# Output-projection weights of a cached-attention decode block loaded in four sets of heads, with attention outputs dealt to the rows by identity products

## The chip, the cores and the metric

The kernel runs on one core of one Trainium2 chip. The metric is the time of one execution in microseconds (us) of device time. A core has a matrix engine (TensorE, "PE" in the profile, with its weight loads shown apart as "PEld"), a vector engine (VectorE, "DVE"), an activation engine (ScalarE, "ACT"), a general engine (GpSimd, "POOL") and a small engine that here only issues transfers (SyncE, "SP"). Sixteen DMA engines carry the transfers between the off-chip memory (HBM) and the on-chip memory: SBUF with 128 partitions, into which DMA can write, and PSUM, into which the matrix engine writes.

## The reference

A decode step of one token for four batch rows: an attention block over a cache, then a gated MLP, each with a normalised input that is scaled, shifted and gated by six vectors made from `c`. Cut to what matters:

```python
B, Sq, D = 4, 1, 512
H, Sk, Dh = 32, 4096, 128

def _A_ref(x, k_cache, v_cache, wq, wo):
    q = (x @ wq).reshape(B, Sq, H, Dh).transpose(0, 2, 1, 3)
    scores = einsum('bhqd,bhkd->bhqk', q, k_cache) * Dh ** (-0.5)
    p = softmax(scores)
    o = einsum('bhqk,bhkd->bhqd', p, v_cache)
    return o.transpose(0, 2, 1, 3).reshape(B, Sq, H * Dh) @ wo

mod = (silu(c) @ w_mod).reshape(4, 6, 1, -1)      # sa, ca, ga, sb, cb, gb
h = layernorm(x) * (1 + ca) + sa
x = x + ga * _A_ref(h, A_k_cache, A_v_cache, A_wq, A_wo)
h = layernorm(x) * (1 + cb) + sb
return x + gb * _B_ref(h, ...)                    # gelu, layernorm, gate, two matmuls
```

All arrays are bf16. The K cache and the V cache have 4 x 32 x 4096 x 128 elements each, 134 MB each. `A_wo` is 4096 x 512, 4.2 MB; the rows of one head are 128 neighbouring rows.

## The kernel before

**Tiling.** The work on the cache is cut into 32 tiles (`NT`). Tile `i` is one batch row `b = i % 4` and one group `g = i // 4` of four heads (`HQ = 4`), so that a K tile `kt` and a V tile `vt` are each 128 partitions x 32 KB, 4 MB. A quarter of the partitions (32) belongs to each of the four heads. Two buffers each of `kt` and `vt` exist; the last V tile takes a buffer of `kt`.

**Per tile.** VectorE multiplies a K tile in place by the query, in two halves (`mult`, line 279). TensorE sums the products over the head dimension by products with the identity into PSUM (`reduce_d`, line 285), VectorE adds the last eight (`sum8`), finds the maximum (`scores`), ScalarE takes the exponential into `pbd`, a block-diagonal arrangement of the probabilities. TensorE multiplies it with the V tile (`pv`, line 354); VectorE picks the wanted blocks (`o_pick`, lines 362 and 366), TensorE turns the result into columns (`o_cols`), and VectorE divides by the softmax sum (`o_scale`, into `oTs`). The softmax sum itself is made by `norm_r`, `norm_a` (TensorE) and `norm_b` (a reciprocal on VectorE).

**The order.** It is written out by hand: the loop at the end of the kernel body issues, for every `i`, the first half of tile `i`, `scores(i - 1)`, `norm_b(i - 2)`, the last steps of tile `i - 3`, the second half of tile `i`, and `pv(i - 2)`. Each engine runs its instructions in that order.

**Transfers.** All large loads are issued by SP, one after the other, on one queue, in this order: `w_mod`, `A_wq`, K 0, K 1, V 0; then in each turn `load_k(i + 2)` after the second `reduce_d` of tile `i` and `load_v(i)` after `pv(i - 2)`. A load waits in SP until its buffer is free. At `i == 2`, when `w_mod` and `A_wq` are used up, the pool that held them is closed and another is opened in the same place; the weights of the output projection go there (line 482 `wo_sb` for the first 28 heads, line 485 `wo_last` for the last four). At `i == 30` the last V tile is loaded in four pieces (`TAIL`), followed by the two MLP weights.

**The output projection before.** The 28 heads of `wo_sb` lie in pairs: two heads have 256 rows of `A_wo`, and partition `p` holds rows `2p` and `2p + 1` of the pair, a run of 2 KB in HBM:

```python
in_=A_wo[0:hl].rearrange("(t p r) n -> p t r n", p=P, r=2)
```

So partition `p` of a pair holds, for the first head, the dimensions `2p` and `2p + 1` if `p < 64`, and of the second head if `p >= 64`. The columns of the attention output have to stand the same way: for a tile of the first seven groups `o_cols` makes four products, each with every second column of `osb`, into 64 partitions, and `norm_b` makes two reciprocals, one per half of the partitions. `oTs` has room for `[2, 2]` values per tile and partition (row `r`, pair `t`). Once a group has its four batch rows, `project` runs `o_proj`: 16 products of 128 x 128 weights with four columns, summed over the four heads, and `add_up` adds the result to `acc` in the next turn. The last group and its weights `wo_last` stand head by head, without pairs.

**The end.** After the loop the last V tile is multiplied piece by piece (`o_last`, line 390) while the residual, the second layer norm and the MLP follow; `gate` (line 585) needs `win_sb`, and the last product needs `wout_sb`.

Of the kernel before, what the change touches and what calls it, by code (L numbers as in the profile page):

```python
# [8 lines left out]
BF16 = mybir.dt.bfloat16  # L9
F32 = mybir.dt.float32  # L10
AF = mybir.ActivationFunctionType
ALU = mybir.AluOpType
AX = mybir.AxisListType
PSUM = bass.MemoryType.PSUM

HQ = 4
KC = 64
RD = 8
TAIL = (64, 32, 16, 16)


@with_exitstack
def kernel(
# [16 lines left out]
    nc = tc.nc  # L40
    P = 128
    B, _, D = A_x.shape
    _, H, SK, DH = A_k_cache.shape
    F = B_w_in.shape[1]
    FH = F // 2
    DJ = D // P
# [3 lines left out]
    NQ = H // HQ  # L50
    NT = B * NQ
    R = P // HQ
# [5 lines left out]
    L = NT - 1  # L58
    BL = B - 1
# [3 lines left out]
    consts = ctx.enter_context(tc.tile_pool(name="consts", bufs=1))  # L63
    kvp = ctx.enter_context(tc.tile_pool(name="kv", bufs=2))
    wk = ctx.enter_context(tc.tile_pool(name="work", bufs=2))
    psum = ctx.enter_context(tc.tile_pool(name="psum", bufs=1, space=PSUM))
# [4 lines left out]
    def ps_sm(shape, dtype=F32):  # L71
        return psum.tile(shape, dtype, name="sm", bufs=3)
# [36 lines left out]
    def load_v(i):  # L109
# [8 lines left out]
    ident_bf = consts.tile([P, P], BF16, name="ident_bf")  # L118
    make_identity(nc, ident_bf)
    ident_f = consts.tile([P, P], F32, name="ident_f")  # L120
# [19 lines left out]
        out=sel32, in_=ident_f.rearrange("p (q r) -> p r q", r=R), axis=AX.X, op=ALU.add  # L140
# [8 lines left out]
    sel4 = consts.tile([P, HQ], F32, name="sel4")  # L149
    idr = ident_f.rearrange("p (c g q) -> p g c q", g=R // HQ, q=HQ)  # L150
    for g in range(G):
        nc.vector.tensor_reduce(out=selg[:, g:g + 1], in_=idr[:, g], axis=AX.XY, op=ALU.add)
    nc.vector.tensor_reduce(
        out=sel4, in_=ident_f.rearrange("p (c b) -> p b c", b=B), axis=AX.X, op=ALU.add
    )
    acc = consts.tile([P, DJ, B], F32, name="acc")
    nc.vector.memset(acc, 0.0)
    x1w = consts.tile([P, DJ, R], F32, name="x1w")
# [3 lines left out]
    for k in range(3):  # L162
        t = consts.tile([P, NJ, HQ], BF16, name=f"pbd{k}")
        nc.gpsimd.memset(t, 0.0)
        pbds.append(t)
    for k in range(2):
        t = psum.tile([P, G, DH], F32, name=f"ops{k}", bufs=1)
# [26 lines left out]
    def normed(pool, src, name, then=None, last=None):  # L194
# [24 lines left out]
        out=sg, in0=cx, scalar1=-60.0, scalar2=-1.0, op0=ALU.max, op1=ALU.mult  # L219
# [6 lines left out]
    def mod_cols(s0, n, dst, m0=0, blocks=False):  # L226
# [21 lines left out]
        out=hs, in0=modA[:, DJ:2 * DJ, :], scalar=1.0, in1=xn, op0=ALU.add, op1=ALU.mult  # L248
# [22 lines left out]
    queries(0)  # L271

    st = {}
    oTs = consts.tile([P, NT, 2, 2], BF16, name="oTs")

    def mult(i, kc):
        kt = kts[i][:, kc * KC:(kc + 1) * KC, :]
# [54 lines left out]
        nc.tensor.matmul(z, lhsT=ones_f, rhs=st.pop((i, "rsb")), start=True, stop=True)  # L332
        st[i, "z"] = z

    def norm_b(i):
        rz = wk.tile([P, 2, 2], F32, name="rz", bufs=3)
        z = st.pop((i, "z"))
        if i // B == NQ - 1:  # L340
            nc.vector.reciprocal(out=rz, in_=z.rearrange("p (r t) -> p r t", t=2))
        else:
            for a in range(2):
                h = slice(64 * a, 64 * (a + 1))
                nc.vector.reciprocal(out=rz[h, 0, :], in_=z[h, a:HQ:2])  # L345
            rz = rz[:, 0:1, :].to_broadcast([P, 2, 2])
        st[i, "rz"] = rz

    def pv(i):
# [20 lines left out]
        st[i, "osb"] = osb  # L370

    def o_cols(i):
        op = ps_sm([P, 2, 2])
        osb = st.pop((i, "osb"))
        if i // B == NQ - 1:
            nc.tensor.matmul(op, lhsT=osb, rhs=sel4, start=True, stop=True)
        else:
            for a in range(2):
                for r in range(2):
                    nc.tensor.matmul(  # L380
                        op[64 * a:64 * (a + 1), r, :], lhsT=osb[:, r:P:2],
                        rhs=sel4[:, a:HQ:2], start=True, stop=True, tile_position=(0, 64 * a),
                    )
        st[i, "op"] = op

    def o_last(i, part):
        if part == 0:
            st[i, "op"] = psum.tile([P, 2, 2], F32, name="qps", bufs=1)
        for k in range(sum(TAIL[:part]), sum(TAIL[:part + 1])):
            nc.tensor.matmul(  # L390
                st[i, "op"], lhsT=vts[i][:, k, :], rhs=pbds[i % 3][:, k, :],
                start=(k == 0), stop=(k == NJ - 1),
            )
# [3 lines left out]
            out=oTs[:, i], in0=st.pop((i, "op")), in1=st.pop((i, "rz")), op=ALU.mult  # L397
        )

    def o_proj(g, b0, b1):  # L400
        wp = ps_sm([P, DJ, b1 - b0])
        for j in range(DJ):
            for q in range(HQ):
                r, t = divmod(q, 2)
                w = wo_last[:, q, :] if g == NQ - 1 else wo_sb[:, g * 2 + t, r, :]
                nc.tensor.matmul(
                    wp[:, j, :], lhsT=w[:, j:D:DJ], rhs=oTs[:, g * B + b0:g * B + b1, r, t],
                    start=(q == 0), stop=(q == HQ - 1),
                )
        return wp  # L410

    def o_add(wp, b0, b1):
        a = acc[:, :, b0:b1]
# [8 lines left out]
    spf = consts.tile([P, 2], F32, name="spf")  # L422
    adds = []

    def project(i):

        if i >= 0 and i % B == BL and i < L:
            adds.append((o_proj(i // B, 0, B), 0, B))

    def add_up():  # L430
        while adds:
            o_add(*adds.pop(0))

    QPLAN = {0: (1, 2), 1: (3, 4, 5), 2: (6, 7)}
    for i in range(NT):
        more = list(QPLAN.get(i, ()))
        mult(i, 0)
        if i >= 1:
            scores(i - 1)
        if i >= 2:  # L440
            norm_b(i - 2)
        add_up()
        if i >= 3:
            o_pick(i - 3)
        reduce_d(i, 0)
        if i >= 3:
            o_cols(i - 3)
        if more:
            queries(more.pop(0))
        mult(i, 1)  # L450
        if i >= 1:
            norm_r(i - 1)
        if i >= 3:
            o_scale(i - 3)
        sum8(i, 0)
        reduce_d(i, 1)
        load_k(i + 2)
        if i >= 1:
            norm_a(i - 1)
        project(i - 3)  # L460
        while more:
            queries(more.pop(0))
        if i >= 2:
            pv(i - 2)
        if i == 0:
            load_v(1)
        elif 2 <= i < L:
            load_v(i)
        if i == 2:
            nc.scalar.dma_start(out=sp_t[:, 0:1], in_=B_w_sp[0:1, 0:1])  # L470
            nc.scalar.dma_start(out=sp_t[:, 1:2], in_=B_b_sp.rearrange("(a b) -> a b", b=1))
            mps = ps_sm([P, 4 * DJ, B])
            mod_cols(2, 3 * DJ, mps)
            mod_cols(5, DJ, mps, 3 * DJ, True)
            nc.vector.tensor_copy(out=modT, in_=mps[:, 0:3 * DJ, :])
            nc.vector.tensor_copy(out=gsT, in_=mps[:, 3 * DJ:, :])
            pre_cm.__exit__(None, None, None)
            wts = tl = ctx.enter_context(tc.tile_pool(name="wts", bufs=1))
            wo_sb = wts.tile([P, H // 2 - 2, 2, D], BF16, name="wo_sb")
            wo_last = wts.tile([P, HQ, D], BF16, name="wo_last")  # L480
            hl = (H - HQ) * DH
            nc.sync.dma_start(
                out=wo_sb, in_=A_wo[0:hl].rearrange("(t p r) n -> p t r n", p=P, r=2)
            )
            nc.sync.dma_start(out=wo_last, in_=A_wo[hl:H * DH].rearrange("(q p) n -> p q n", p=P))
        if i == 5:
            sps = ps_sm([P, 2])
            nc.tensor.matmul(sps, lhsT=ones_b, rhs=sp_t, start=True, stop=True)
            nc.vector.tensor_copy(out=spf, in_=sps)
            nc.vector.tensor_scalar(  # L490
                out=gwT, in0=gsT, scalar1=spf[:, 0:1], scalar2=None, op0=ALU.mult
            )
            nc.vector.tensor_scalar(
                out=gsT, in0=gsT, scalar1=spf[:, 1:2], scalar2=None, op0=ALU.mult
            )
            nc.vector.tensor_copy(out=g8[:, :, 1, :], in_=gwT.rearrange("p j b -> p b j"))
            cbT = modT[:, 2 * DJ:3 * DJ, :]
            nc.vector.tensor_scalar_add(out=cbT, in0=cbT, scalar1=1.0)
        if i == L - 1:
            load_v(L)  # L500
            win_sb = wts.tile([P, DJ, F], BF16, name="win_sb")
            nc.sync.dma_start(out=win_sb, in_=B_w_in.rearrange("(p j) n -> p j n", p=P))
            wout_sb = wts.tile([P, NH, D], BF16, name="wout_sb")
            nc.sync.dma_start(out=wout_sb, in_=B_w_out.rearrange("(j p) n -> p j n", p=P))
# [13 lines left out]
    o_pick(L - 1)  # L518
    o_cols(L - 1)
    o_scale(L - 1)  # L520
    adds.append((o_proj(NQ - 1, 0, BL), 0, BL))
    add_up()
    o_last(L, 0)


# [3 lines left out]
    def sums():  # L529
# [2 lines left out]
        o_scale(L)  # L532

    xc, rs2 = normed(tl, x1, "ln2", lambda: o_last(L, 1), sums)
    wp = o_proj(NQ - 1, BL, B)
    last = tl.tile([P, DJ], F32, name="last")
    nc.vector.tensor_tensor(out=last, in0=wp[:, :, 0], in1=gaT[:, :, BL], op=ALU.mult)
    xs = st2[:, 0, 0:DJ]
# [13 lines left out]
        out=nv2, in0=mq2[:, 0:1], scalar=mq2[:, 0:1], in1=mq2[:, 1:2],  # L552
        op0=ALU.mult, op1=ALU.subtract,
# [4 lines left out]
    hl = tl.tile([P, DJ], F32, name="hl")  # L558
    nc.vector.scalar_tensor_tensor(
        out=hl, in0=xs, scalar=mq2[:, 0:1], in1=cbT[:, :, BL], op0=ALU.subtract, op1=ALU.mult  # L560
    )
    nc.vector.scalar_tensor_tensor(
        out=hT2[:, :, BL], in0=hl, scalar=rsl, in1=sbT[:, :, BL], op0=ALU.mult, op1=ALU.add
# [4 lines left out]
        out=x1m, in0=x1[:, :, :, None].to_broadcast([P, DJ, B, HQ]),  # L568
        in1=mask4[:, None, None, :].to_broadcast([P, DJ, B, HQ]), op=ALU.mult,
    )  # L570
    x1r = ps_sm([B * DJ, P])
    for k in range(DJ):
        nc.tensor.matmul(
            x1r[:, k:P:DJ], lhsT=x1m[:, k].rearrange("p b j -> p (b j)"), rhs=sel32,
            start=True, stop=True,
# [4 lines left out]
    def gate(h):  # L580
# [22 lines left out]
        in1=st3[:, 0:2], op=ALU.mult,  # L603
# [72 lines left out]
```

## Time and profile before

| what | value |
|---|---|
| time, median of 3 runs | 670.07 us (669.81 to 670.64) |
| the profiled execution | 671.33 us |
| its span, first to last instruction | 669.5 us |
| busy: PE, PEld, DVE, ACT, POOL | 403.3, 181.8, 421.1, 85.0, 3.8 us |
| read from HBM | 282.73 MB, 422 GB/s over the span |
| granted TensorE clock, mean | 0.828 |

The profile is of one execution. It has a page and answers to further questions. On the page, part 2 cuts the span into 40 equal slices: a digit is the busy share of a slice in tenths, and under `DMA` it is the mean of the 16 DMA engines; `GB/s` is what they moved. Part 3 lists the DMA queues with packets, MB and the share of the sixteen engines' time. Part 4, the chain, follows the work that ended last backwards from step to step and gives the share of each engine and line. Part 5 has the groups of instructions: line, engine, operation, output and inputs, count, then busy time, mean ns of one, idle time before and its cause. A line `L285` is line 285 of the kernel. The table of stretches gives for each stretch its length, busy time (and instruction count) of PE, PEld, DVE, ACT and POOL, the granted clock, the DMA share and GB/s. The timeline gives start, duration, engine, line, operation and, in brackets, the idle time before it and what ended it. The trace also records every DMA packet with its size and how long it took.

### The profile page before, as it was taken

How to read it: one execution, taken by the hardware profiler on the slowest of the kernel's cores; microseconds unless marked ns; L12 is line 12 of the kernel's file. 1: busy time of each engine (PE TensorE's matmuls, PEld its weight loads, DVE VectorE, ACT ScalarE, POOL GpSimd, SP SyncE). 2: the span in 40 equal slices, each digit the busy share in tenths (PEclk: the TensorE clock that was granted, in tenths of full speed). 3: DMA queues.
4: the chain of work that ended last, by engine and by line, in shares of the span. 5: the costliest groups of instructions: out<-in, count | busy, mean ns of one | idle time of the engine just before them, and what ended most of it. 6: DMA issues, size and time to landing. Idle time of an engine off the chain costs nothing.

```text
span 669.5 us, 7043 instructions
## 1 busy us (share of the span) xinstructions
PE 403.3 (60%) x2920; PEld 181.8 (27%) x2920; DVE 421.1 (63%) x614; ACT 85.0 (13%) x278; POOL 3.8 (1%) x17
## 2 busy tenths in 40 slices
PE   1185886365676576557655664675565467555666
PEld 1032432122232232223222222232222233222325
DVE  3186494765666776666677665567766666776833
ACT  1011111110111111001111100111111011111112
POOL 1000000000000000000000000000000000000000
PEclk9999877678888777898877689878778897877975
DMA  9999999999999999999999999999999999999994
GB/s 376 437 426 435 400 404 418 433 439 428 430 433 434 435 432 431 432 435 434 430 433 431 434 434 433 430 431 432 437 432 435 426 436 433 435 434 422 435 422 198
DMA packets 13555, 283.18 MB, mean 423 GB/s; under 512 B 1228, under 2 KB 2644, under 8 KB 4692
## 3 DMA queue, kind: packets, MB, share of 16 engines
q1 hardware_dynamic: 13504, 282.73, 98.6%
q8 instruction: 23, 0.38, 0.2%
q14 instruction: 8, 0.07, 0.0%
q10 hardware_dynamic: 20, 0.01, 0.0%
HBM read 282.73 MB, written 0.00 MB: 422 GB/s over the span
## 4 chain that ended last, share of the span: by engine, by line
DMA 58%; DVE 28%; PE 13%; issue 1%; SPq 0%; ACT 0%; DVEq 0%
DMA kt<-in_A_k_cache_dram 52%; DVE kt L279 20%; PE red L285 11%; DMA win_sb<-in_B_w_in_dram 5%; DVE osb L366 2%; DVE S L294 1%; DVE osb L362 1%; DVE mrow L303 1%; PE ops L354 1%; DVE rz L345 1%; DVE mt L307 0%; PE qps L265 0%; DVE nM L309 0%; DVE mb L305 0%; DVE nM L310 0%
## 5 line engine op out<-in xcount | busy, mean ns | idle before, releaser
L285 PE MATMUL red<-kt,ident_bf 128*128 128x512 bf16 x1024 | 302.3, 461 | 234.7 <-DVE kt L279 234.7
L279 DVE TENSOR_TENSOR kt<-kt,qbc 128x8192 bf16<-128x8192 bf16 x64 | 282.8, 4420 | 191.7 <-DMA kt<-in_A_k_cache_dram 190.7
L285 PEld LDWEIGHTS <-ident_bf 128*128 128x128 bf16 x1024 | 116.3, 114 | 408.7 <-issue 284.9
L317 ACT ACTIVATE pbd<-S,nM 32x128 bf16<-32x128 f32 x128 | 73.8, 576 | 504.9 <-DVE nM L310 463.6
L354 PE MATMUL ops<-vt,pbd 128*16 128x512 bf16 x992 | 60.7, 387 | 0.2 <-DMA vt<-in_A_v_cache_dram 0.2
L294 DVE TENSOR_REDUCE S<-red 128x64 f32<-128x512 f32 x64 | 43.7, 682 | 6.3 <-PE red L285 6.3
L366 DVE SCALAR_TENSOR_TENSOR osb<-ops,selg,osb 128x128 f32<-128x128 f32 x93 | 32.6, 351 | 3.3
L317 ACT ACTIVATION_READ_ACCUMULATOR pbd<-S,nM 32x1 f32 x128 | 32.0, 250 | 0.0
L354 PEld LDWEIGHTS <-pbd 128*16 128x16 bf16 x992 | 22.5, 90 | 23.4 <-issue 1.8
L265 PE MATMUL qps<-wq_sb,hTb 128*32 128x512 bf16 x128 | 9.2, 412 | 9.2 <-DMA wq_sb<-in_A_wq_dram 8.5
L332 PEld LDWEIGHTS sm<-rsb,ones_f 128*128 128x128 f32 x64 | 12.3, 194 | 4.5
L362 DVE TENSOR_SCALAR osb<-ops,selg 128x128 f32<-128x128 f32 x31 | 10.8, 348 | 4.3 <-PE ops L354 3.6
L380 PEld LDWEIGHTS sm<-sel,osb 128*64 128x64 f32 x224 | 9.2, 138 | 11.9 <-issue 11.4
L380 PE MATMUL sm<-sel,osb 128*64 128x2 f32 x224 | 11.6, 205 | 0.0
L269 ACT CAST qbc<-qps 128x512 bf16<-128x512 f32 x8 | 4.7, 586 | 48.3 <-PE qps L265 48.3
L303 DVE TENSOR_REDUCE mrow<-S 128x1 f32<-128x128 f32 x32 | 9.2, 286 | 1.1
L345 DVE RECIPROCAL rz<-sm 64x2 f32<-64x2 f32 x56 | 9.1, 163 | 0.4
L332 PE MATMUL sm<-rsb,ones_f 128*128 128x4 f32 x64 | 9.3, 215 | 0.0
L325 DVE TENSOR_SCALAR rsb<-mask,rs 128x4 f32<-128x4 f32 x32 | 7.1, 223 | 2.4 <-ACT pbd L317 2.4
L307 DVE STREAM_TRANSPOSE mt<-mb 128x32 f32<-128x32 f32 x32 | 6.8, 212 | 1.1
L265 PEld LDWEIGHTS <-hTb 128*32 128x32 bf16 x128 | 3.0, 99 | 13.3 <-issue 10.6
L309 DVE TENSOR_REDUCE nM<-mt 128x1 f32<-128x32 f32 x32 | 6.0, 186 | 1.1
(125 smaller groups left out, 84.4 us busy)
## 6 DMA issues: line engine op xcount, KB each, us to landing
kt<-in_A_k_cache_dram SPq DMA_DIRECT2D x31, 4096.0 KB, 22.6
vt<-in_A_v_cache_dram SPq DMA_DIRECT2D x31, 4096.0 KB, 30.3
wq_sb<-in_A_wq_dram SPq DMA_DIRECT2D x1, 4096.0 KB
kt<-in_A_k_cache_dram SPq DMA_DIRECT2D x2, 2048.0 KB, 20.3
wo_sb<-in_A_wo_dram SPq DMA_DIRECT2D x1, 3584.0 KB, 29.3
wm_sb<-in_w_mod_dram SPq DMA_DIRECT2D x1, 3072.0 KB, 10.4
kt<-in_A_v_cache_dram SPq DMA_DIRECT2D x1, 2048.0 KB
win_sb<-in_B_w_in_dram SPq DMA_DIRECT2D x1, 1792.0 KB, 33.9
```

The costliest lines, as they stand in the source:

```text
L265: nc.tensor.matmul(qp[R * q:R * (q + 1)], lhsT=hTb[:, k, b, :], rhs=wq_v[:, k, gs, q, :], start=(k == 0), stop=(k == DJ - 1), tile_positio ...
L279: nc.vector.tensor_tensor(out=kt, in0=kt, in1=bc(qbc[:, g, b, :], KC), op=ALU.mult)
L285: nc.tensor.matmul(red, lhsT=ident_bf, rhs=kt[:, :, m * RD:(m + 1) * RD], start=(m == 0), stop=(m == DH // RD - 1),)
L294: nc.vector.tensor_reduce(out=st[i, "S"][:, kc * KC:(kc + 1) * KC], in_=st.pop((i, "red", kc)), axis=AX.X, op=ALU.add,)
L303: nc.vector.tensor_reduce(out=mrow, in_=S, axis=AX.X, op=ALU.max)
L317: nc.scalar.activation(out=pbd[r, :, q], in_=S[r, :], func=AF.Exp, bias=nM[r, :], scale=att_scale, accum_out=rs[r, :],)
L332: nc.tensor.matmul(z, lhsT=ones_f, rhs=st.pop((i, "rsb")), start=True, stop=True)
L345: nc.vector.reciprocal(out=rz[h, 0, :], in_=z[h, a:HQ:2])
L354: nc.tensor.matmul(opss[i % 2][g:g + G * HQ], lhsT=pbds[i % 3][:, n, :], rhs=vts[i][:, n, :], start=(m < 4), stop=(m >= NJ // G - 4), tile ...
L362: nc.vector.tensor_scalar(out=osb, in0=ops[:, 0, :], scalar1=selg[:, 0:1], scalar2=None, op0=ALU.mult)
L366: nc.vector.scalar_tensor_tensor(out=osb, in0=ops[:, g, :], scalar=selg[:, g:g + 1], in1=osb, op0=ALU.mult, op1=ALU.add,)
L380: nc.tensor.matmul(op[64 * a:64 * (a + 1), r, :], lhsT=osb[:, r:P:2], rhs=sel4[:, a:HQ:2], start=True, stop=True, tile_position=(0, 64 * a),)
```

## The change

`A_wo` of the first 28 heads is loaded in four sets of 8, 8, 8 and 4 heads, each by its own transfer. Within a set of `s` heads partition `p` holds rows `s * p` to `s * p + s - 1` of the set, one run of 8 KB, or 4 KB for the last set. For a set of 8 heads, 16 partitions hold one head. `oTs` now holds each tile's output simply by head, `o_cols` is one product, and `norm_b` one reciprocal.

When the last tile of a set is done (tiles 7, 15, 23 and 27), `deal` moves the outputs to the partitions that hold their weight rows: for each quarter `q` of the partitions and each row `r`, a product with 32 columns picked from the identity matrix (`picks`) into 32 partitions of PSUM. With two heads per quarter both heads are multiplied and land beside each other, and `dealt`, on VectorE in the next turn, keeps the right one in each half (`half` is a 0/1 mask) and writes `od`. `project` then runs the 128 x 128 products with `od`, over the 8 (or 4) rows instead of over the four heads, later in that turn, and `add_up` follows a turn after that. So the four sets are projected at `i` = 11, 19, 27 and 31 instead of seven groups at `i` = 6, 10, 14 ... 30. The last group, `wo_last` and the end are as before. Three constants are new in SBUF: `half`, `pick1` and `pick2`. They take 32, 256 and 512 bytes of every partition, and all that is placed behind them moves up: the first `kt` begins at byte 35360 of its partition instead of 34560, and `vt`, `wo_sb` and `win_sb` move by 800 to 864 bytes too.

```diff
+SETS = (8, 8, 8, 4)
...
+    half = consts.tile([P, 2], F32, name="half")
+    nc.vector.tensor_reduce(
+        out=half, in_=ident_f.rearrange("p (q a u) -> p a q u", a=2, u=R // 2), axis=AX.XY, op=ALU.add
+    )
...
-    oTs = consts.tile([P, NT, 2, 2], BF16, name="oTs")
+    oTs = consts.tile([P, NT, HQ], BF16, name="oTs")
...
     def norm_b(i):
-        rz = wk.tile([P, 2, 2], F32, name="rz", bufs=3)
-        z = st.pop((i, "z"))
-        if i // B == NQ - 1:
-            nc.vector.reciprocal(out=rz, in_=z.rearrange("p (r t) -> p r t", t=2))
-        else:
-            for a in range(2):
-                h = slice(64 * a, 64 * (a + 1))
-                nc.vector.reciprocal(out=rz[h, 0, :], in_=z[h, a:HQ:2])
-            rz = rz[:, 0:1, :].to_broadcast([P, 2, 2])
+        rz = wk.tile([P, HQ], F32, name="rz", bufs=3)
+        nc.vector.reciprocal(out=rz, in_=st.pop((i, "z")))
...
     def o_cols(i):
-        op = ps_sm([P, 2, 2])
-        osb = st.pop((i, "osb"))
-        if i // B == NQ - 1:
-            nc.tensor.matmul(op, lhsT=osb, rhs=sel4, start=True, stop=True)
-        else:
-            for a in range(2):
-                for r in range(2):
-                    nc.tensor.matmul(
-                        op[64 * a:64 * (a + 1), r, :], lhsT=osb[:, r:P:2],
-                        rhs=sel4[:, a:HQ:2], start=True, stop=True, tile_position=(0, 64 * a),
-                    )
+        op = ps_sm([P, HQ])
+        nc.tensor.matmul(op, lhsT=st.pop((i, "osb")), rhs=sel4, start=True, stop=True)
...
+    ends, picks = {}, {}
+    h0 = 0
+    for k, hs_ in enumerate(SETS):
+        h0 += hs_
+        ends[h0 // HQ * B - 1] = k
...
+    for n in (1, 2):
+        picks[n] = consts.tile([P, n * HQ, R], BF16, name=f"pick{n}")
+        for a in range(n):
+            u = R // n
+            nc.vector.tensor_copy(
+                out=picks[n][:, :, a * u:(a + 1) * u],
+                in_=ident_bf.rearrange("p (u r) -> p r u", r=n * HQ),
+            )
+
+    def deal(k):
+        s_, h0 = SETS[k], sum(SETS[:k])
+        n = s_ // HQ
+        pp = ps_sm([P, s_, B, n])
+        for q in range(HQ):
+            g, a = divmod(h0 + n * q, HQ)
+            for r in range(s_):
+                nc.tensor.matmul(
+                    pp[R * q:R * (q + 1), r], lhsT=picks[n][:, r, :], rhs=oTs[:, g * B:(g + 1) * B, a:a + n],
+                    start=True, stop=True, tile_position=(0, R * q),
+                )
+        st["pp"] = pp, k
+
+    def dealt():
+        if "pp" in st:
+            pp, k = st.pop("pp")
+            s_ = SETS[k]
+            od = wk.tile([P, s_, B], BF16, name="od", bufs=1)
+            if s_ == HQ:
+                nc.vector.tensor_copy(out=od, in_=pp[:, :, :, 0])
+            else:
+                nc.vector.tensor_scalar(
+                    out=od, in0=pp[:, :, :, 0], scalar1=half[:, 0:1], scalar2=None, op0=ALU.mult
+                )
+                nc.vector.scalar_tensor_tensor(
+                    out=od, in0=pp[:, :, :, 1], scalar=half[:, 1:2], in1=od,
+                    op0=ALU.mult, op1=ALU.add,
+                )
+            st["od"] = od, k
+
+    def project():
+        if "od" in st:
+            od, k = st.pop("od")
+            wp = ps_sm([P, DJ, B])
+            for j in range(DJ):
+                for r in range(SETS[k]):
+                    nc.tensor.matmul(
+                        wp[:, j, :], lhsT=wo_sb[:, sum(SETS[:k]) + r, j:D:DJ], rhs=od[:, r, :],
+                        start=(r == 0), stop=(r == SETS[k] - 1),
+                    )
+            adds.append((wp, 0, B))
...
-    def project(i):
-
-        if i >= 0 and i % B == BL and i < L:
-            adds.append((o_proj(i // B, 0, B), 0, B))
...
         add_up()
+        dealt()
         if i >= 3:
             o_pick(i - 3)
...
-        project(i - 3)
+        project()
+        if i - 3 in ends:
+            deal(ends[i - 3])
...
-            wo_sb = wts.tile([P, H // 2 - 2, 2, D], BF16, name="wo_sb")
+            wo_sb = wts.tile([P, H - HQ, D], BF16, name="wo_sb")
...
-            nc.sync.dma_start(
-                out=wo_sb, in_=A_wo[0:hl].rearrange("(t p r) n -> p t r n", p=P, r=2)
-            )
+            h0 = 0
+            for n in SETS:
+                nc.sync.dma_start(
+                    out=wo_sb[:, h0:h0 + n, :],
+                    in_=A_wo[h0 * DH:(h0 + n) * DH].rearrange("(p r) n -> p r n", p=P),
+                )
+                h0 += n
```

More of the change, by code (lines that the diff above doesn't have):

```diff
@@ L387, in o_last @@
         if part == 0:
-            st[i, "op"] = psum.tile([P, 2, 2], F32, name="qps", bufs=1)
+            st[i, "op"] = psum.tile([P, HQ], F32, name="qps", bufs=1)
         for k in range(sum(TAIL[:part]), sum(TAIL[:part + 1])):
@@ L398, in o_scale, with o_proj @@
         )
-    def o_proj(g, b0, b1):
+    def o_proj(b0, b1):
         wp = ps_sm([P, DJ, b1 - b0])
+        i0 = (NQ - 1) * B
         for j in range(DJ):
             for q in range(HQ):
-                r, t = divmod(q, 2)
-                w = wo_last[:, q, :] if g == NQ - 1 else wo_sb[:, g * 2 + t, r, :]
                 nc.tensor.matmul(
-                    wp[:, j, :], lhsT=w[:, j:D:DJ], rhs=oTs[:, g * B + b0:g * B + b1, r, t],
+                    wp[:, j, :], lhsT=wo_last[:, q, j:D:DJ], rhs=oTs[:, i0 + b0:i0 + b1, q],
                     start=(q == 0), stop=(q == HQ - 1),
@@ L410, in o_proj @@
         return wp
+    ends, picks = {}, {}
[3 more added lines that the diff above has]
+        ends[h0 // HQ * B - 1] = k
+    assert h0 == H - HQ
+    for n in (1, 2):
[45 more added lines that the diff above has]
+            adds.append((wp, 0, B))
     def o_add(wp, b0, b1):
@@ L520 @@
     o_scale(L - 1)
-    adds.append((o_proj(NQ - 1, 0, BL), 0, BL))
+    adds.append((o_proj(0, BL), 0, BL))
     add_up()
@@ L534 @@
     xc, rs2 = normed(tl, x1, "ln2", lambda: o_last(L, 1), sums)
-    wp = o_proj(NQ - 1, BL, B)
+    wp = o_proj(BL, B)
     last = tl.tile([P, DJ], F32, name="last")
```

## The prediction

> **What bounds the kernel now.** I read the page's slices first, then its queues, the chain, the waits, and the table of stretches around the changed load. Rows of parts 2 and 3 of the page:
>
> ```profile
> DMA  9999999999999999999999999999999999999994
> GB/s 376 437 426 435 400 404 418 433 439 428 430 433 434 435 432 431 432 435 434 430 433 431 434 434 433 430 431 432 437 432 435 426 436 433 435 434 422 435 422 198
> DMA packets 13555, 283.18 MB, mean 423 GB/s; under 512 B 1228, under 2 KB 2644, under 8 KB 4692
> q1 hardware_dynamic: 13504, 282.73, 98.6%
> ```
>
> All sixteen DMA engines are busy from the first slice to the last but one, at about 433 GB/s, and SP's queue has 98.6% of their time. The kernel is a stream of 282.73 MB plus a short end. Slices 5 and 6 (67 to 100 us) are slower than their neighbours.
>
> The chain and the list of waits:
>
> ```profile
> DMA 58%; DVE 28%; PE 13%; issue 1%; SPq 0%; ACT 0%; DVEq 0%
> DMA kt<-in_A_k_cache_dram 52%; DVE kt L279 20%; PE red L285 11%; DMA win_sb<-in_B_w_in_dram 5%; DVE osb L366 2%; DVE S L294 1%; DVE osb L362 1%; DVE mrow L303 1%; PE ops L354 1%; DVE rz L345 1%; DVE mt L307 0%; PE qps L265 0%; DVE nM L309 0%; DVE mb L305 0%; DVE nM L310 0%
> ```
> ```profile
> DVE kt L279 <- DMA kt<-in_A_k_cache_dram: 190.7, 29, 17.3
> ```
>
> The chain names DVE and PE because a K load is issued when PE has freed its buffer. But a K load lands a median 22.6 us after its issue (part 6), and its 4.19 MB take 9.7 us at 433 GB/s: some 13 us are queueing. VectorE waits for K tiles 29 times, 190.7 us in all. The compute engines have room; the queue has none. So an edit counts by the DMA time it saves or adds.
>
> The stretches around the load of `wo_sb` (the last two columns are the DMA share and GB/s):
>
> ```profile
> 84.00:96.00 12.00, 9.31 (x36) 3.77 (x36) 11.69 (x18) 2.31 (x8) 0.00 (x0) 0.70 1.01 433
> 96.00:112.00 16.00, 12.42 (x78) 5.25 (x76) 10.95 (x17) 2.32 (x8) 0.00 (x0) 0.79 1.04 392
> 112.00:300.00 188.00, 111.52 (x737) 48.32 (x736) 119.86 (x161) 20.81 (x72) 0.00 (x0) 0.81 1.00 432
> ```
>
> From 96 to 112 us the engines are as busy as ever and move 392 GB/s: (1 - 392/433) x 16 = 1.5 us lost. In it lie the 2 KB packets of `wo_sb` and the 1 KB packets of `wo_last`.
>
> **The change, part by part.**
>
> *The weight load.* `wo_sb` is 28 x 128 rows of 1 KB, 3.67 MB: 1792 packets of 2 KB. On the trace's packet records these take a median 86 ns and a mean 89.9 ns: 1792 x 86 / 16 = 9.63 us of the queue (10.07 by the mean, which counts overlap at both edges twice). After it they are 384 packets of 8 KB and 128 of 4 KB. The last V tile alone has these sizes in this queue: 309 and 159 ns in every one. 384 x 309 / 16 + 128 x 159 / 16 = 7.42 + 1.27 = 8.69 us. Gain 0.94 us by medians, 1.38 by the mean. By bytes: of the 1.5 us lost, `wo_last` has 512 x 48 / 16 = 1.54 us less 0.524 MB / 433 GB/s = 1.21 us, that is 0.33; `wo_sb` lost 1.2, and the new packets lose 8.69 - 3.67 MB / 433 GB/s = 0.21. Gain 1.0 us, which I take, since bytes count no overlap. Ends: 0.94 and 1.38.
>
> All later loads stand behind this one in the same queue, and none of them waits for a buffer long enough to let it run dry (13 us of queueing for K; a V load lands 30.3 us after issue). So the whole stream moves forward.
>
> *Four transfers instead of one.* Three more issues on SP at 0.38 to 0.43 us, and three more ends. SP at that place:
>
> ```profile
> 80.93 0.38 SPq L482 DMA_DIRECT2D wo_sb<-in_A_wo_dram  x1
> 81.36 19.93 SPq L485 DMA_DIRECT2D wo_last<-in_A_wo_dram  x1
> 101.46 2.41 SPq L101 DMA_DIRECT2D kt<-in_A_k_cache_dram  x1
> ```
>
> SP sits 19.93 us in the issue of `wo_last`, behind 1792 packets, and K 5 goes out at 101.46 although PE freed its buffer at 97 (its last sums of K 3 run from 93.47 for 3.61 us). With 512 packets SP should be free sooner. Either way K 5 starts behind `wo_last`, near 110 us: 0. Gaps between transfers: at the end the four pieces of the last V tile and the MLP weights follow each other, 417 GB/s from 646 to 657 us; 11 x (1 - 417/433) = 0.4 us over five joints with all smaller packets in it. For three joints between 0 and 0.24 us; the packet durations above already come from such pieces, so 0.
>
> [...]
>
> *`norm_b`.* 56 reciprocals of 163 ns become 28 of about 170 (row L341, 128 x 4): VectorE loses 4.4 us of work. *`o_cols`.* 28 x 4 products become 28; PE loses some 12 + 9 us of overlapped time. Both lie where the engine next waits for a K tile: 0.
>
> *`deal`.* 3 x 32 + 16 = 112 new products of 32 columns. Sixteen projection products take 0.65 us in a row (156.69 us), so a set costs 0.65 to 1.3 us, twice that at half clock. Behind it on PE stand `pv(i - 2)`, and behind that SP's V load: covered by the 20 us a V load queues (30.3 - 9.7). Projection itself has 112 products as before, 32 at a time. 0.
>
> *`dealt`.* Six VectorE operations, below the 351 ns of row L366, and one copy, in turns 11, 19, 27, 31: at most 0.7 us in a turn in which VectorE then waits about 6 us for K. 0. If that cover were gone, each turn would cost 0.7.
>
> *Start.* One reduction (0.37 us like L139) and three copies (L253: 0.43) on VectorE. It idles 17.31 us before the first K tile. 0.
>
> *The end.* The sum of the last set moves from 628.40 us to behind `norm_r(L)` at 643.89, 0.17 us on VectorE ahead of `osb`, which PE awaits. PE's next steps there wait for DMA anyway:
>
> ```profile
> 646.88 3.59 PE L354 MATMUL ops<-vt,pbd 128*16 128x512 bf16 x32 [0.21 <-DMA vt<-in_A_v_cache_dram]
> 657.45 0.59 PE L390 MATMUL qps<-pbd,kt 128*128 128x4 bf16 x16 [0.64 <-DMA kt<-in_A_v_cache_dram]
> 662.00 1.66 PE L585 MATMUL red<-hT,win_sb 128*128 128x4 bf16 x56 [0.68 <-DMA win_sb<-in_B_w_in_dram]
> ```
>
> 0.17 is under the first wait, and the second (0.64) takes what is left: 0. All three waits are for loads that move forward together; the 7.5 us behind `win_sb` stay.
>
> *Code.* PE has 224 more rows, DVE 7. Queue q8 fetches instructions in 23 packets; each takes about 0.93 us (0.2% x 669.5 x 16 / 23). One more: 0.06 us on the mean engine, 0.93 at worst if it meets the engine that ends last.
>
> Sum: 671.33 (span 669.5 and 1.8 around it) - 1.0 + 0.06 = 670.4 for a profiled execution. That one stands 1.26 above the median of 670.07; against the median, **669.1 us**.
>
> **The rivals.** Measured differences under 0.2%, 1.34 us, are not told from none.
>
> *A. The engine that ends last gains more.* In the last slices the sixteen engines finish over some 6 us (share 0.50 from 657 to 665 us), and `win_sb` lands with the latest. If the code fetches fall on other engines, that one gains 0.93 more: 1.0 to 1.38 + 0.93, 668.2 in the middle, 667.8 at best. For: 23 fetches, unevenly spread. Against: it can as well go the other way (671.0).
>
> *B. Nothing arrives.* If a V or K load starts late once, as at 76 to 84 us, where 369 GB/s mean 1.2 us lost because K 4 was issued at 76 us into a queue nearly empty, the gain is given back: 670.1. For: it happens once here. Against: nothing ahead of 80 us changes order.
>
> *C. Slower: the moved buffers.* By the built programs' addresses `kt` and `vt` begin at multiples of 256 bytes now (34560) and 32 past one after (35360). A 32 KB packet takes 1213 ns and a 16 KB packet 611, so 2 x 611 - 1213 = 9 ns are fixed per packet. If a shifted start makes a packet pay that twice, 528 such packets per engine cost 4.75 us: 673.8. It decides from 1.8 ns a packet. For: no row here has such a start. Against: `A_wq` lands 128 bytes past a multiple of 256 with the same 1213 ns.
>
> [...]
>
> **How the numbers follow.** Forecast (gain of 0.5 to 1.33) 0.43, its own range 668.7 to 669.6; A 0.29; B 0.08; C 0.20. Faster by over 0.2% is A alone, 0.29; within 0.2% the forecast and B, 0.51; slower C, 0.20. The range goes from A's best, 667.8, to the fetch on the last engine with no gain, 671.0; most of C lies outside.
>
> **What would show it.** No 2 KB packets; under 8 KB some 1600 fewer. From 96 to 111 us above 420 GB/s, and SP out of `wo_last` well before 101 us. K 6 and all later tiles about 1 us earlier, `win_sb` near 661 us, the end behind it as long as now. Single packets of 32 KB still at 1213 ns: if they take 1215 or more, C holds. If VectorE waits for something other than K at `i` = 11, 19 or 27, a cover named above is gone. Wrong altogether if `win_sb` does not move with the stream.

## The result, and the profile after

The changed kernel takes 672.17 us (median of 11 runs, 671.71 to 674.51) beside 670.13 us (11 runs, 669.69 to 672.01) for the kernel before: a ratio of 1.0027 [1.0016, 1.0039]. It is 2.0 us slower. The forecast was 669.1 us and no change, the range ended at 671.0, and rival C (the moved buffers) had a chance of 0.20. The profiled execution of the changed kernel took 671.79 us, with a span of 670.0 us.

Parts 2 and 3 of the page of the kernel after, the rows that the prediction began with:

```profile
DMA  9999999999999999999999999999999999999995
GB/s 376 432 432 425 430 418 426 435 434 427 426 435 431 431 428 427 433 430 431 428 433 430 432 426 431 435 426 430 434 430 432 426 431 430 429 432 423 439 413 203
DMA packets 12322, 283.17 MB, mean 423 GB/s; under 512 B 1276, under 2 KB 2692, under 8 KB 3076
q1 hardware_dynamic: 12272, 282.73, 98.6%
```

The same bytes go in fewer packets: 3076 under 8 KB instead of 4692, 1616 fewer, as forecast. The queue still has 98.6% of the engines' time. Slices 5 and 6 (67 to 100 us) move 430 and 418 GB/s instead of 400 and 404. But the long middle of the kernel, slices 11 to 35, where the row of before mostly shows 430 to 437, now mostly shows 426 to 433: 20 of these 25 slices are a little slower, in places that the change doesn't touch.

The stretches of the kernel after (length; busy time and instructions of PE, PEld, DVE, ACT, POOL; granted clock; DMA share; GB/s):

```profile
76.00:84.00 8.00, 3.94 (x100) 2.82 (x93) 4.02 (x3) 0.59 (x1) 0.00 (x0) 0.90 0.98 416
96.00:112.00 16.00, 12.50 (x100) 5.49 (x100) 9.47 (x16) 2.31 (x8) 0.00 (x0) 0.89 1.03 423
112.00:300.00 188.00, 102.70 (x685) 47.01 (x678) 118.18 (x153) 20.82 (x72) 0.00 (x0) 0.83 1.00 430
300.00:612.00 312.00, 184.61 (x1216) 84.18 (x1216) 201.21 (x263) 37.03 (x128) 0.00 (x0) 0.84 1.00 430
```

and of the kernel before, the two stretches that the prediction didn't show:

```profile
76.00:84.00 8.00, 4.86 (x113) 3.23 (x113) 3.10 (x3) 0.59 (x1) 0.00 (x0) 0.82 0.97 369
300.00:612.00 312.00, 188.74 (x1248) 82.79 (x1248) 206.35 (x278) 37.00 (x128) 0.00 (x0) 0.83 1.00 433
```

The load of the weights (96 to 112 us) became faster: 423 instead of 392 GB/s, 16 x 31 / 433 = 1.1 us won. From 112 to 612 us the stream runs at 430 instead of 432 and 433 GB/s with a DMA share of 1.00 in both: 188 x 2/432 + 312 x 3/433 = 0.9 + 2.2 = 3.0 us lost. The engines are not idle; the same packets last longer. The two spans differ by only 0.5 us, in part since the profiled execution of before let its queue run nearly dry at 76 to 84 us (369 GB/s, the 1.2 us of the prediction), and that of after did not (416). Medians of many executions are therefore the better comparison: 2.0 us.

The records of the single packets show what lasts longer. One DMA engine of the kernel after, its packets of 32 KB from the third on (13.0 us), in ns (as far as 75 us):

```
1213 1213 1213 1213 1213 1213 1213 1213 1213 1213 1213 1213 1213 1213 1213 1213 1213 1213 1213 1213
1215 1216 1221 1215 1216 1224 1216 1216 1216 1224 1214 1215 1224 1216 1216 1216 1224 1216 1214 1224
1216 1216 1216 1224 1216 1216 1221 1215 1216 1216 1224 1216
```

In the kernel before this row is 1213 all along. In the kernel after it is 1213 for the first 20 to 24 packets of every engine, to about 37 us, and then a repeating pattern of 1216, 1216, 1216, 1224. Behind 113 us (packets over 1240 ns, which were held up by something else, left out) the mean is 1217.9 instead of 1213.0. The kernel has some 7,700 packets of 32 KB behind the first ones: 4.9 ns x 7,700 / 16 = 2.4 us. The smaller packets last longer too: 16 KB 615.5 for 611 ns, 8 KB 314.4 for 309, 4 KB 162 for 159, 1 KB a median 47 for 46; with those of 14 KB that is some 0.5 us. So 2.9 us are added; with the 0.8 us that the weight load wins by itself (e3 and e4, below) that is 2.1, and 2.0 were measured.

SP around the weight load, in the timeline of the kernel after:

```profile
80.01 1.75 SPq L530 DMA_DIRECT2D wo_sb<-in_A_wo_dram  x4
81.80 0.43 SPq L535 DMA_DIRECT2D wo_last<-in_A_wo_dram  x1
95.91 0.33 SPq L103 DMA_DIRECT2D kt<-in_A_k_cache_dram  x1
```

The issue of `wo_last` takes 0.43 us instead of 19.93, and K 5 goes out at 95.91 us, when its buffer is free, instead of at 101.46.

### The profile page after: what moved, and what is told of

It is laid out like the page before. It is cut to its first block, busy times and chain, and to the rows that moved or that the text cites. A ratio compares the mean times of both kernels' runs of the same rounds, so it can differ in the third digit from the quotient of the medians.

```text
span 670.0 us, 6859 instructions
## 1 busy us (share of the span) xinstructions
PE 388.6 (58%) x2864; PEld 182.6 (27%) x2864; DVE 415.3 (62%) x594; ACT 85.0 (13%) x278; POOL 3.8 (1%) x17
## 2 busy tenths in 40 slices
DMA packets 12322, 283.17 MB, mean 423 GB/s; under 512 B 1276, under 2 KB 2692, under 8 KB 3076
## 3 DMA queue, kind: packets, MB, share of 16 engines
q1 hardware_dynamic: 12272, 282.73, 98.6%
## 4 chain that ended last, share of the span: by engine, by line
DMA 58%; DVE 28%; PE 12%; issue 1%; SPq 0%; DVEq 0%
DMA kt<-in_A_k_cache_dram 53%; DVE kt L286 21%; PE red L292 10%; DMA wout_sb<-in_B_w_out_dram 5%; DVE osb L364 2%; DVE S L301 1%; DVE mrow L310 1%; DVE osb L360 1%; PE ops L352 1%; DVE mt L314 0%; DVE nM L316 0%; PE qps L272 0%; DVE mb L312 0%; DVE nM L317 0%; PE sm L240 0%
## 5 line engine op out<-in xcount | busy, mean ns | idle before, releaser
L292 PE MATMUL red<-kt,ident_bf 128*128 128x512 bf16 x1024 | 292.1, 450 | 251.3 <-DVE kt L286 251.3
L352 PEld LDWEIGHTS <-pbd 128*16 128x16 bf16 x992 | 24.1, 90 | 21.6 <-issue 1.7
L372 PEld LDWEIGHTS sm<-sel,osb 128*128 128x128 f32 x62 | 11.9, 198 | 11.1 <-DVE osb L364 4.5
L372 PE MATMUL sm<-sel,osb 128*128 128x4 f32 x62 | 9.3, 221 | 5.4 <-DVE osb L364 5.4
L312 DVE COPY mb<-mrow 128x32 f32<-128x32 f32 x32 | 5.8, 181 | 1.1
```

What stands on the lines that cost most here:

```text
L292: nc.tensor.matmul(red, lhsT=ident_bf, rhs=kt[:, :, m * RD:(m + 1) * RD], start=(m == 0), stop=(m == DH // RD - 1),)
L352: nc.tensor.matmul(opss[i % 2][g:g + G * HQ], lhsT=pbds[i % 3][:, n, :], rhs=vts[i][:, n, :], start=(m < 4), stop=(m >= NJ // G - 4), tile ...
L372: nc.tensor.matmul(op, lhsT=st.pop((i, "osb")), rhs=sel4, start=True, stop=True)
```

## The experiments

The theory after the result: `kt` and `vt` begin 32 bytes past a multiple of 256 bytes, and that alone makes their packets longer. The rivals: the new instructions cost the time (`deal`, `dealt` and the rest on an engine that matters), or the four transfers do. The edits change the length of `oTs`, which nothing reads beyond its first `NT` entries, or put in an unused tile, and so move what lies behind. "Start" is the first byte of `kt` and `vt`, and of the weights loaded later, modulo 256, by the addresses of the built programs. The kernel before has 0 and 128, the kernel after 32 and 224.

| kernel | start of K and V | start of weights | median, us | ratio to before [95%] | 32 KB packet, mean ns |
|---|---|---|---|---|---|
| before | 0 | 128 | | 1 | 1213.0 |
| after | 32 | 224 | 672.17 | 1.0027 [1.0016, 1.0039] | 1217.9 |
| e1: before, moved by 32 | 32 | 160 | 673.35 | 1.0049 [1.0036, 1.0061] | 1217.9 |
| e2: before, moved by 64 | 64 | 192 | 672.96 | 1.0045 [1.0032, 1.0058] | 1216.8 |
| e3: after, aligned | 0 | 192 | 669.21 | 0.9986 [0.9978, 0.9995] | 1213.0 |
| e4: e3, weights in one transfer | 0 | 192 | 670.02 | 1.0001 [0.9992, 1.0011] | 1213.0 |
| e5: before, moved by 128 | 128 | 0 | 671.12 | 1.0023 [1.0010, 1.0036] | 1216.6 |
| e6: before, only V moved | K 0, V 32 | 160 | 670.53 | 1.0010 [1.0000, 1.0020] | 1214.2 |
| e8: e3, weights aligned too | 0 | 0 | 669.21 | 0.9986 [0.9976, 0.9997] | 1213.0 |
| e9: before, weights aligned | 0 | 0 | 669.67 | 0.9995 [0.9986, 1.0005] | 1213.0 |

The packet means are all taken as above, behind 113 us.

### e1, e2: the kernel before, with its buffers moved

```diff
-    oTs = consts.tile([P, NT, 2, 2], BF16, name="oTs")
+    oTs = consts.tile([P, NT + 4, 2, 2], BF16, name="oTs")
```

(e2: `NT + 8`.)

> The kernel before with its buffer oTs 32 bytes per partition longer, and nothing else: every tile behind it (kt, vt, the weights) begins 32 bytes higher, as it does in the changed kernel, no instruction differs. Start theory: DMA into a tile that begins 32 bytes past a multiple of 64 is slower, because 32 KB packets went from 1213 ns to some 1217 on average; 8064 of them on 16 engines make 2.2 us, with the smaller packets 2.4 to 2.6: 672.6 us against 670.1, and the packet records show 1214 to 1224 ns from about 36 us on. Work theory (the four transfers or the added products cause it): 670.1, all packets at 1213.

> The kernel before with oTs 64 bytes longer, so kt and vt begin 64 bytes past a multiple of 256. Start theory on a grid of 64 bytes: 670.1, packets at 1213. Start theory on a grid of 128 or 256 bytes: 672.6 as with 32. Work theory: 670.1.

Measured: 673.35 and 672.96 us beside 670.02, that is 3.3 and 2.9 us for a move of 32 or 64 bytes with not one instruction changed. Stretches of e1:

```profile
96.00:112.00 16.00, 12.41 (x78) 5.23 (x77) 10.81 (x17) 2.32 (x8) 0.00 (x0) 0.79 1.04 390
112.00:300.00 188.00, 108.96 (x736) 47.88 (x734) 119.34 (x161) 20.80 (x72) 0.00 (x0) 0.82 1.00 431
300.00:612.00 312.00, 194.09 (x1248) 83.94 (x1248) 204.02 (x277) 37.01 (x128) 0.00 (x0) 0.81 1.00 430
```

The weight load is as slow as before (390), the K and V stream as slow as after (431 and 430). The 32 KB packets leave 1213 ns behind 25 to 28 packets on 15 of the 16 engines and show the same pattern (e2: behind 27 to 32, mostly 1215 and 1222 ns). The start of the buffers is the cause by itself; the new instructions are not needed for it. And e1 is 1.2 us slower than after, of which the weight load wins 0.8 (e3 and e4); the rest isn't told from noise.

### e3, e4: the kernel after, with its buffers aligned, and without its weight load

```diff
-    oTs = consts.tile([P, NT, HQ], BF16, name="oTs")
+    oTs = consts.tile([P, NT + 28, HQ], BF16, name="oTs")
```

e4 has this too, and loads the weights as the kernel before does:

```diff
-            h0 = 0
-            for n in SETS:
-                nc.sync.dma_start(
-                    out=wo_sb[:, h0:h0 + n, :],
-                    in_=A_wo[h0 * DH:(h0 + n) * DH].rearrange("(p r) n -> p r n", p=P),
-                )
-                h0 += n
+            nc.sync.dma_start(
+                out=wo_sb.rearrange("p (t r) n -> p t r n", r=2),
+                in_=A_wo[0:hl].rearrange("(t p r) n -> p t r n", p=P, r=2),
+            )
```

> The changed kernel with oTs 224 bytes longer: kt and vt begin at multiples of 256 again, with all the change's work and transfers kept. Start theory: the 2.5 us go and the gain of the weight load remains: 669.1 us (1.0 under before), packets at 1213. Work theory: stays at 672.2.

> As the run before it, but wo_sb loaded by one transfer in runs of 2 KB as in the kernel before; the weights then stand in an order that the projection does not expect, only the time is meant. Start theory with the gain from packet size: 670.1, that is 1.0 above the run before it; 375 to 392 GB/s around 100 us. If the size of the runs is worth nothing: equal to the run before it.

Measured: 669.21 and 670.02 us beside 670.02. Stretches of e3:

```profile
96.00:112.00 16.00, 12.49 (x76) 5.52 (x78) 9.96 (x16) 2.32 (x8) 0.00 (x0) 0.79 1.01 417
112.00:300.00 188.00, 108.51 (x712) 48.48 (x713) 119.85 (x157) 20.84 (x72) 0.00 (x0) 0.82 1.00 433
300.00:612.00 312.00, 184.75 (x1218) 83.90 (x1217) 202.17 (x264) 37.00 (x128) 0.00 (x0) 0.83 1.00 432
```

and the first of them in e4:

```profile
96.00:112.00 16.00, 12.49 (x73) 5.52 (x71) 10.17 (x16) 2.32 (x8) 0.00 (x0) 0.79 1.03 394
```

With aligned buffers the stream is back at 433 and 432 GB/s, its packets at 1213.0 ns, and the change does what its first step said: 0.8 us faster than before [0.3, 1.5 by the ratio's interval]. e4 separates the parts: with the load of before and everything else of the change (`deal`, `dealt`, `o_cols`, `norm_b`, the constants) the time is that of before to 0.1%. So these parts cost nothing that can be measured, and the load gives all of the 0.8 us.

### e5, e6: what is the grid, and which tiles pay

e5 is e1 with `NT + 16`. e6 moves only the V tiles:

```diff
     load_k(1)
+    kvp.tile([P, 8], F32, name="gap", bufs=1)
     load_v(0)
```

> The kernel before with oTs 128 bytes longer: kt and vt begin 128 bytes past a multiple of 256, the weights at a multiple of 256. Start theory on a grid of 128 bytes: 670.0 us, 32 KB packets at 1213 ns. On a grid of 256 bytes: 672.5 to 673.4 as with 32 and 64, packets at 1214 to 1224.

> The kernel before with a gap of 32 bytes between the kt and the vt buffers: K tiles stay at multiples of 256, V tiles and the weights begin 32 bytes past one. The last V tile takes a kt buffer. Start theory with the price on each packet into a shifted tile: 31 of 64 tiles, half of the 3.0 us that 32 bytes cost on all: 671.5. If only K tiles matter, because VectorE writes into them: 670.0. If the price is all or nothing: 673.

Measured: e5 671.12 us beside 670.21, with 32 KB packets of 1216.6 ns; 64 bytes past a multiple of 256 gave 1216.8 (e2). The time is below the 672.5 to 673.4 us expected and rises 1.5 us less than in e2 (by the ratios, whose intervals overlap). A part of this can be the weights, which move to a multiple of 256 in it: their 2 KB packets take a median 84 ns instead of 86, the 1 KB packets all 46, and 96 to 112 us moves 417 GB/s instead of the 394 of e2, 16 x 23 / 433 = 0.85 us. In e9 below, where only the weights are aligned, the gain of the whole isn't told from none; so why e5 is cheaper than e2 stays open. Stretches of e5:

```profile
96.00:112.00 16.00, 12.42 (x101) 5.55 (x103) 9.96 (x17) 2.33 (x8) 0.00 (x0) 0.89 1.04 417
112.00:300.00 188.00, 109.55 (x716) 47.46 (x709) 120.82 (x162) 20.80 (x72) 0.00 (x0) 0.80 1.00 431
300.00:612.00 312.00, 193.78 (x1248) 83.90 (x1248) 204.61 (x276) 36.97 (x128) 0.00 (x0) 0.81 1.00 431
```

e6: 670.53 us, only 0.3 us above before [0.0, 1.3], and a mean packet of 1214.2 ns; 27% of the packets last longer than 1213. With half of the tiles moved, less than half of the price is paid (1.2 of 4.9 ns). A price paid by each moved packet by itself would have given 2.4 ns.

### e7: what switches it on

The late start of the longer packets (about 37 us in the kernel after) could have been the start of the compute engines, which use SBUF too, or the identity of the first tiles. e7 is e1 with the loads at the start in another order, K 0 last:

```diff
-    load_k(0)
-    load_k(1)
     load_v(0)
+    for i in range(2):
+        kts[i] = kvp.tile([P, NJ, DH], BF16, name="kt", bufs=2)
+    for i in (1, 0):
+        load(kts[i], kv_view(A_k_cache, i), (NJ,))
```

> The kernel before with all tiles 32 bytes higher, and at the start the loads in the order V 0, K 1, K 0 instead of K 0, K 1, V 0, so that the products on VectorE and TensorE begin near 50 us instead of 31. DMA-alone theory: on every engine the packets leave 1213 ns after 26 to 28 packets of 32 KB as in the first run with 32 bytes, near 42 us, before any product. Engine theory (the compute engines' accesses to shifted tiles slow the DMA writes): all packets at 1213 until the products begin near 50 us.

One execution, 690.37 us: the first tile comes late, and the queue runs dry meanwhile. A line of the timeline of e7, and one of its stretches:

```profile
49.80 4.43 DVE L281 TENSOR_TENSOR kt<-kt,qbc 128x8192 bf16<-128x8192 bf16 x1 [36.79 <-DMA kt<-in_A_k_cache_dram]
```
```profile
50.00:60.00 10.00, 5.72 (x14) 1.98 (x14) 8.56 (x2) 0.00 (x0) 0.00 (x0) 1.00 0.01 2
```

The 32 KB packets of one engine of e7 from its third on (12.8 us), to about 96 us:

```
1213 1213 1213 1213 1213 1213 1213 1213 1213 1213 1213 1213 1213 1213 1213 1213 1213 1213 1213 1213 1213 1213 1213 1213
1216 1225 1216 1216 1216 1224    (pause of the queue)    1841 1211
1213 1213 1213 1213 1213 1213 1213 1213 1213 1213 1213 1213 1213 1213 1213 1213 1213 1213 1213 1213 1213 1213
```

The packets become longer at about 42 us, 8 us before VectorE's first product on a K tile, so the start of the work on the tiles isn't the cause. After a pause from 49.2 to 66.1 us, in which the queue moves hardly anything (2 GB/s from 50 to 60 us, 0 from 60 to 66), the packets of the same moved buffers take 1213 ns again, 24 or more in a row on 14 of the 16 engines. On the other two the longer packets came back earlier, each time right behind an instruction fetch on that engine (16 KB at 86 us, 8 KB at 68 us); on a third one behind such a fetch at 100 us, and on most of the rest behind the 1 KB packets of `wo_last`, at 127 us. From 130 us the mean is 1217.9 again. So neither the tile nor its address alone decides: packets into the same moved buffers took 1213 ns behind the pause and 1217.9 later.

### e8, e9: the weights aligned as well

e8 is e3 with `wk.tile([P, 16], F32, name="gap", bufs=1)` ahead of `oTs`, e9 is the kernel before with

```diff
+    wk.tile([P, 32], F32, name="gap", bufs=1)
     st = {}
```

> The changed kernel with oTs 224 bytes longer and a gap of 64 bytes behind it, so that kt and vt and also all weights (wo_sb, wo_last, win_sb, wout_sb) begin at multiples of 256. Start theory on a grid of 256 bytes: 32 KB packets at 1213, 1 KB packets at 46 ns instead of up to 59, so 0.2 to 0.4 us under the run with only kt and vt on the grid: 668.9 us. If the weights' start is worth nothing: 669.2.

> The kernel before with a gap of 128 bytes between the V buffers and the weights, so that the weights begin at multiples of 256 and kt and vt stay there; wo_sb in runs of 2 KB as before. Start theory: 2 KB packets at 84 ns and 1 KB packets at 46 as in the run with 128 bytes, 0.4 to 0.7 us less: 669.5 us, so about half of what the larger runs gain. If the start of the weights is worth nothing: 670.2.

Measured: e8 669.21 us beside 669.63 (0.9986), no better than e3. e9 669.67 beside 669.63 (0.9995): its load of the weights moves 413 instead of 392 GB/s in the stretch 96 to 112 us, its 2 KB packets take a median 84 instead of 86 ns, and its 1 KB packets 46; but a gain of the whole isn't told from none. The weights are 7 MB of 283, so there is little to win. The change with aligned buffers (e3 or e8) is the fastest kernel here.

## Why the prediction was wrong

**The step that failed** is the reading of rival C: "Against: `A_wq` lands 128 bytes past a multiple of 256 with the same 1213 ns." `A_wq`'s packets are the first eight of 32 KB on each engine, and the first 20 take 1213 ns in every kernel here, moved or not. K 0 of the kernel after, 32 bytes off, takes 1213 ns too. The row was a true measurement of a state that holds for some 27 us out of 650. So it could not exclude C, and its use as the main evidence against C is what gave C 0.20 and the forecast an unchanged packet.

**The size of C** was wrong as well, in the other direction. 9 ns were priced by supposing that a packet pays its fixed part twice; 4.9 were measured. By the terms of the sum: gain 1.0 (0.8 measured, e3 against e4 and before), C 4.75 (2.4 for the 32 KB packets and some 0.5 for smaller ones, most of which C didn't count; e1 3.3 in all). Starts 32, 64 and 128 bytes past a multiple of 256 cost 4.9, 3.8 and 3.6 ns for each 32 KB packet behind 113 us (e1, e2, e5), the first packets nothing. C's 673.8 was 1.6 us too high, the forecast 3.1 too low. The threshold, 1.8 ns a packet, was passed, and the sign that the prediction gave ("if they take 1215 or more, C holds") is what the records show: median 1216.

Point by point:

- *The weight load*: 0.94 to 1.38 us forecast, 0.8 measured (e3 against e4, 669.21 and 670.02), a little under the low end. Right within noise. In the kernel after its 8 and 4 KB packets took a mean 314.4 and 162 ns rather than 309 and 159. That `wo_sb` begins 224 bytes past a multiple of 256 does not explain this by itself: in e3 it begins at 192, K and V at 0, and these packets take a median 309 and 159 ns.
- *Four transfers instead of one*: SP left the issue of `wo_last` after 0.43 us, as forecast, and K 5's earlier issue still queues behind `wo_last`. What that issue is worth no run separates from the 0.8 us of the load. Three more transfers in the queue add no time that shows: e3 with four (8 and 4 KB packets) took 669.21 us, e4 with one (2 KB) 670.02. Right as far as shown.
- *"So the whole stream moves forward"*: it did by 0.8 us in e3, and was then held back in the kernel after by 4.9 ns in each packet. PE waits there for `win_sb` until 662.35 us (662.00 before), not 661:

```profile
662.35 1.65 PE L635 MATMUL red<-hT,win_sb 128*128 128x4 bf16 x56 [0.61 <-DMA win_sb<-in_B_w_in_dram]
```

- *The end*: the 7.5 us behind `win_sb` were to stay; they are 670.0 - 662.35 = 7.65. Right. In e3 the wait for `win_sb` is gone and the end waits for VectorE, which the prediction had not said:

```profile
659.31 1.63 PE L635 MATMUL red<-hT,win_sb 128*128 128x4 bf16 x56 [0.17 <-DVE hT L612]
```

- *`norm_b`, `o_cols`, `deal`, `dealt`, the start*, all costed at 0: right, e4 is 1.0001 [0.9992, 1.0011]. Groups of the kernel after:

```profile
L425 PE MATMUL sm<-oTs,pick 128*32 128x8 bf16 (+1 forms) x112 | 2.4, 168 | 0.0
...
L344 DVE RECIPROCAL rz<-sm 128x4 f32<-128x4 f32 x32 | 5.5, 173 | 0.3 <-PE sm L339 0.3
```

and the first `dealt` after a set, in its timeline:

```profile
242.78 0.22 DVE L439 TENSOR_SCALAR od<-sm,half 128x32 bf16<-128x32 f32 x1
243.03 0.25 DVE L442 SCALAR_TENSOR_TENSOR od<-sm,half,od 128x32 bf16<-128x32 f32 x1
```

  112 products of `deal` and 0.47 us of `dealt` a turn, as reckoned. The cover is still there: ahead of the K tiles of the turns with `dealt` VectorE waits 6.61, 6.80, 6.62 and 1.79 us, for K each time, and in the list of waits of the kernel after it waits for K even longer than before (190.7 us).

```profile
DVE kt L286 <- DMA kt<-in_A_k_cache_dram: 201.0, 29, 16.9
```

- *Code*: one more fetch was forecast (0.06 us); the queue of instructions has 22 packets instead of 23. The step counted the new rows and not those that go (`o_cols`, `norm_b`): the kernel after has 6859 instructions in its profile, that of before 7043. Wrong, and of no weight.
- *Rival A* (the last engine gains more) and *rival B* (a late load gives the gain back) were not needed. B's pause at 76 to 84 us is in the profiled run of before, not in that of after, which is why two profiles alone would have hidden three quarters of the loss.

## What to carry to other kernels

When a kernel is bound by its loads, look at where in SBUF the streamed buffers begin before and after every edit, even one that only adds a few constants: here starts of K and V 32, 64 and 128 bytes past a multiple of 256 cost 0.2 to 0.5% of the whole (1.0023 to 1.0049), several times what the edit was worth, and an unused tail of 224 bytes in another tile brought it back. A single row that speaks against a mechanism counts only if it is in the state that holds for most of the run; compare packets from the middle of the stream, not its first ones. And where two profiles differ by less than the medians, find the pause that one of them caught.

## What was not expected of the hardware

- The price of a moved start was paid per packet more than per byte: in the kernel after 4.9 ns of 1213 for 32 KB, 4.5 of 611 for 16 KB, 5.4 of 309 for 8 KB, 3 of 159 for 4 KB. It differed little between 32 and 128 bytes off (1217.9 and 1216.6 ns).
- It had a grace: 20 to 24 packets of 32 KB per engine in the kernel after, and on most engines 25 to 28 in e1, 27 to 32 in e2, 42 to 56 in e5 (where `A_wq`'s eight are aligned). The grace came back after the pause in the queue of e7, with 24 or more packets of 1213 ns on 14 of the 16 engines. No run here shows the mechanism, and it stays open. That the start of the buffers is the cause, and its price, don't depend on it.
- A few moved transfers among aligned ones did not pay: in e3, with the weights 192 bytes off, the packets of `wo_sb` take a median 309 and 159 ns and the 14 KB ones of `win_sb` 535, as in e8, where they are aligned. In the kernel after, where K and V are moved as well, they take 313, 161 and 539.
- The issue of one transfer held SP for 19.93 us behind 1792 queued packets of 2 KB, and for 0.43 us behind 512 of 8 and 4 KB.
